# A memory-attention and FFN kernel: the second product of batches 2 to 7 in Strassen's form for every second pair of k blocks

## The chip, the cores and the metric

The kernel runs on one core of one Trainium2 chip. The metric is the device time of one execution in microseconds (us). The profile names the core's engines PE (TensorE: matrix products), PEld (its weight loads), DVE (VectorE), ACT (ScalarE), POOL (GpSimd) and SP (SyncE, which here only issues DMAs).

## What is computed

The inputs are q, k and v (8 batches, 8 heads, 576 tokens, 64 numbers a head), phi (32 memory slots a head) and two weight matrices, 512x2048 and 2048x512.

```python
a = phi - np.max(phi, axis=2, keepdims=True)
a = np.exp(a)
a = a / (np.sum(a, axis=2, keepdims=True) + 1e-09)
k_m = np.einsum('bhsm,bhsd->bhmd', a, k)
v_m = np.einsum('bhsm,bhsd->bhmd', a, v)
...
attn = attn / (np.sum(attn, axis=-1, keepdims=True) + 1e-09)
return np.matmul(attn, v_m).astype(np.float32)
...
h = x @ w_in
sp = np.maximum(h, 0.0) + np.log1p(np.exp(-np.abs(h)))
g = h * erf(sp)
return (g @ w_out).astype(np.float32)
```

x holds the attention's result, 4608 tokens by 512. `h = x @ w_in` is the first product and `g @ w_out` the second.

## The kernel before

**Stages.** The batches are worked off one after the other. For each, the kernel sums k and v under phi to 32 slots a head, and multiplies the slots of v with `w_in` beforehand (`vw`), so that the first product (`ffn1`) multiplies the softmax weights (`at`) of 256 slots with `vw`. Its 2048 columns are cut in 16 blocks k of 128, so that there are 128 steps (b, k) over the 8 batches.

**A step.** For one block k, `ffn1` makes h for the 576 tokens in two halves of 288 (`psh`); each half is copied from PSUM to SBUF by DVE or ACT (`h`). ACT makes softplus and erf (`e`), four steps at a time because each function needs its own table. `g_split` (L909) multiplies e by h on DVE (L932), rounds the result to `g_hi` (L934), keeps the rounding error as `g_lo` (L935), and POOL copies the last 64 tokens aside (L939). `ffn2` (L947) multiplies g with the rows k of `w_out`, which lie in SBUF as `wo` in a high and a low part; there are four blocks of 128 tokens, each with a PSUM bank (`pso0` to `pso3`) in which it sums over k.

**Three matmuls for a product.** A product of fp32 accuracy is made of three matmuls of the rounded parts (`products`, L843): high by high, high by low, low by high. So a block of 128 tokens takes three matmuls of 128x512 for each k.

**What is left of 576.** 576 is four times 128 and 64 more. `ffn2_rest` (L970) multiplies the last 64 tokens of two batches together, as one more block (`psr`), 16 k by three matmuls for each of four pairs of batches, 192 matmuls in all. The last block of the last batch is cut in two halves of 256 columns at its end (`last_block`, L988, `psy`).

**What sets the order.** The program is recorded as operations with a rank and with buffers from pools; `Plan.order` (L133) plays them through with a planned cost for each and writes the instructions of every engine in the order that results. A table at the end of the function shifts the ranks of single operations. On the chip each engine takes its instructions in that order, and waits where an input is not there. SP does the same with DMAs: a DMA whose buffer is not free holds up all that stand behind it.

**Pools.** h and e have five buffers each, `g_hi` and `g_lo` three each, the PSUM tiles of the first product share four banks (`ps`) with the attention's. `w_in` lies in SBUF for good (`w_in0` to `w_in3`, 1 MB each).

Of the kernel before, what the change touches and what calls it, by code (L numbers as in the profile page):

```python
# [250 lines left out]
def tile_memory_attention_then_erf_softplus_ffn(  # L251
# [22 lines left out]
    NB = U // 32  # L274
    NPR = DFF // 256
    NK = DFF // P
    NS = B * NK
    NT = S // P
    REST = S - NT * P
    NC = phi.shape[2]  # L280
    ROWS = [min(ROW, S - c * ROW) for c in range(NC)]
# [5 lines left out]
    ORDER = [(b, k) for b in range(B) for k in range(NK)]  # L287
    GROUPS = [4] * (NS // 4 - 1) + [2, 2]
    LAG = 6
# [4 lines left out]
    TAIL = 3  # L294
# [3 lines left out]
        for n, b, kw in (  # L298
            ("const", 1, {}),
            ("wo", NPR, {}),  # L300
            ("vw", 2, {}),
            ("att", 1, {}),
            ("at", 8, {}),
            ("small", 2, {}),
            ("el", 5, {}),
            ("g", 3, {}),
# [7 lines left out]
    room = {"wo": NPR, "vw_hi": 2, "vw_lo": 2, "at": 8, "h": HB, "e": EB}  # L314
    room.update({"g_hi": 3, "g_lo": 3, "raw": RAW, "ps": 4, "sc": 2, "dk": 1, "bias": 1, "phiT": 2, "row": 2})
# [6 lines left out]
        "h": ("el", [P, S], F32),  # L322
        "e": ("el", [P, S], F32),
        "sc": ("att", [P, NG, U], F32),
# [3 lines left out]
        **{n: ("small", [P, NG * NB], F32) for n in ("smx", "ssm", "srs")},  # L328
# [3 lines left out]
    def tile_(tag, *key, shape=None, dtype=F32, pool=None):  # L332
        key = plan.tile(tag, *key)
        p, s, d = SHAPES.get(tag, (pool, shape, dtype))
        T[key] = lambda: pools[p].tile(s, d, name=key[0], tag=tag, bufs=BUFS.get(tag))
        return key
# [21 lines left out]
    rest = const.tile([P, NK, 2, P], F32R, name="rest")  # L358
# [59 lines left out]
    def load_kv(rank, b, x, g):  # L418

        key = tile_("raw", "kv", b, x, g, shape=[P, NC, 4 * D], pool="raw")  # L420
        src = kv[b - 1, 2 * g + x] if b else kv_0[x, g]
        load(rank, P * NC * 4 * D * 4, [key], lambda: queue(b, g if x == 0 else 0).dma_start(out=get(key), in_=src))

    def load_q(rank, u):
        b, hf = divmod(u, 2)
        src = qT[b, hf].rearrange("r (p s) -> r p s", p=NP_)
        if u < 2:
            key = tile_("wo", "q", u, shape=[P, NP_, U], pool="wo")
            load(rank, P * NP_ * U * 4, [key], lambda: nc.sync.dma_start(out=get(key), in_=src))
            return  # L430
        for x in range(2):
            key = tile_("at", "q", u, x, shape=[P, 2, U], pool="at")
            load(rank, P * 2 * U * 4, [key], lambda x=x, key=key: nc.sync.dma_start(
                out=get(key), in_=src[:, 2 * x : 2 * x + 2]))
# [4 lines left out]
    def q_of(u, rows, p):  # L439
        return get(("q", u))[rows, p] if u < 2 else get(("q", u, p // 2))[rows, p % 2]  # L440

    wo, wf, raw_of = {}, {}, {}

    def decode(rank, name, c):
# [17 lines left out]
        if name == "in":  # L462
            dst = ("w_in", c)
# [5 lines left out]
        def merge():  # L469
            t, v = word(1), word(0)  # L470
            if name == "in":
                at_ = c % 2 * f
                to = w_in_sb[c // 2][:, :, at_ : at_ + f]
# [162 lines left out]
    def sums_and_turn(rank, b, part, rank_2=None, into=None):  # L636
# [11 lines left out]
        def sums_of(n):  # L648
# [4 lines left out]
            return get(banks[n])[:, U : U + n_x * D]  # L653
# [116 lines left out]
    def vw(rank, b, k, n, exact):  # L770
# [7 lines left out]
        ws = [(("w_in", k // 2), k % 2)] if n == 1 else [("w_in", c) for c in range(k // 2, (k + n) // 2)]  # L778
# [3 lines left out]
               lambda: of_heads(ps, vm[b % 2], lambda rows, p: w_in_sb[i][rows, p, cols]))  # L782
# [12 lines left out]
    def attention(rank, rank_2, u, more=0):  # L795
        b = u // 2
        s = tile_("sc", "sc", u)
        ps = heads(U + more, "sc", u)
        yield
        yield (4 * U / 2.4, [("km", b % 2)] + q_keys(u), [(k, "sc") for k in ps], [s],  # L800
               lambda: of_heads(ps, km[b % 2], lambda rows, p: q_of(u, rows, p), U))
# [4 lines left out]
        def wide(k):  # L806
            return get(k).unsqueeze(2).to_broadcast([P, NG * NB, M])

        for g in range(NG):
            op(DVE, on_dve(U), rank, [(ps[g], "sc")], [(s, g)], lambda g=g: nc.vector.transpose(  # L810
                out=get(s)[:, g, :], in_=get(ps[g])[:, :U]))
        mx, sm, rs = (tile_(n, n, u) for n in ("smx", "ssm", "srs"))
        op(DVE, on_dve(S), rank_2, [s], [mx], lambda: nc.vector.reduce_max(
            out=get(mx), in_=view(), axis=AX.X))
        op(DVE, on_dve(S), rank_2, [s, mx], [s], lambda: nc.vector.tensor_tensor(
            out=view(), in0=view(), in1=wide(mx), op=ALU.subtract))
        op(ACT, on_act(S), rank_2, [s], [s],
           lambda: nc.scalar.activation(get(s), get(s), AF.Exp, scale=SCALE if b >= TURNED else 1.0),
           kind="exp")
        op(DVE, on_dve(S), rank_2, [s], [sm], lambda: nc.vector.reduce_sum(  # L820
# [4 lines left out]
        op(DVE, on_dve(S), rank_2, [s, rs], [s], lambda: nc.vector.tensor_tensor(  # L825
            out=view(), in0=view(), in1=wide(rs), op=ALU.mult))
        shape = [P, NG, U]
        if u < 2:
            to = tile_("at", "at", u, shape=shape, pool="at")
        else:  # L830
            to = tile_("sc", "f", u)
        op(DVE, on_dve(S), rank_2, [s], [to], lambda: nc.vector.transpose(
# [4 lines left out]
    def at_split(rank, u, src):  # L837
        hi = tile_("at", "at_hi", u, shape=[P, NG, U], dtype=F32R, pool="at")
        lo = tile_("at", "at_lo", u, shape=[P, NG, U], dtype=F32R, pool="at")
        split(rank, hi, lo, src, S, lambda: get(hi), lambda: get(lo), lambda: get(src))  # L840
# [7 lines left out]
    def ffn1(rank, i, half):  # L848
# [5 lines left out]
        h = ("h", i)  # L854
        if i < IN_PSUM:
            ps = tile_(f"pso{half + 1}", "psh", i, half)
        else:
            if half == 0:
                tile_("h", *h)
# [19 lines left out]
        def keep():  # L879
            return get(h)[:, half * U : (half + 1) * U]  # L880

        op(DVE, on_dve(U), rank - 20, [ps], [(h, half)],
# [9 lines left out]
    def softplus(rank, i, edge):  # L892
        e = tile_("e", "e", i)
        if i < IN_PSUM:
            for x, (half, ps) in enumerate(halves_of(i)):
                last[:] = [op(ACT, on_act(U, True), rank, [ps], [(e, x)],
                              lambda half=half, ps=ps: nc.scalar.activation(
                                  get(e)[:, half], get(ps)[:, :U], AF.Softplus),
                              kind="softplus", edge=edge and x == 1, after=last)]
            return  # L900
        last[:] = [op(ACT, on_act(S), rank, [("h", i)], [e], lambda: nc.scalar.activation(  # L901
            get(e), get(("h", i)), AF.Softplus), kind="softplus", edge=edge, after=last)]

# [351 lines left out]
```

## Time and profile before

| what | value |
|---|---|
| time of three runs | 695.98 us median (695.84 to 696.05) |
| span of the profiled execution, first to last instruction | 694.3 us |
| what the median has beyond that span | 1.7 us |
| PE busy | 686.9 us, 99% |
| DVE busy | 460.5 us, 66% |
| ACT busy | 488.9 us, 70% |
| POOL busy | 117.0 us, 17% |
| DMA | 67.37 MB, 97 GB/s in the mean |

The profiled execution has no separate time of its own; its span is set against the median of the runs, which lie within 0.2 us. Busy times are unions of instruction spans. A matmul's span is longer than the distance to the next one, since they are pipelined, so that the distance from start to start, not the span, tells what a matmul costs in a row of them.

### The profile page before, as it was taken

How to read it: one execution, taken by the hardware profiler on the slowest of the kernel's cores; microseconds unless marked ns; L12 is line 12 of the kernel's file. 1: busy time of each engine (PE TensorE's matmuls, PEld its weight loads, DVE VectorE, ACT ScalarE, POOL GpSimd, SP SyncE). 2: the span in 40 equal slices, each digit the busy share in tenths (PEclk: the TensorE clock that was granted, in tenths of full speed). 3: DMA queues.
4: the chain of work that ended last, by engine and by line, in shares of the span. 5: the costliest groups of instructions: out<-in, count | busy, mean ns of one | idle time of the engine just before them, and what ended most of it. 6: DMA issues, size and time to landing. Idle time of an engine off the chain costs nothing.

```text
span 694.3 us, 12260 instructions
## 1 busy us (share of the span) xinstructions
PE 686.9 (99%) x4813; PEld 558.5 (80%) x4813; DVE 460.5 (66%) x807; ACT 488.9 (70%) x773; POOL 117.0 (17%) x262
## 2 busy tenths in 40 slices
PE   8999999999999999999999999999999999999998
PEld 4565778888887888888888888878888888888886
DVE  4999999678853587674863648774775346744560
ACT  3899999975876568867665776885576655757641
POOL 0021323132210222111111102111111011110120
PEclk9999999999999999999999999999999999999999
DMA  9999231624202151125211142110010100010002
GB/s 361 417 415 416 91 103 43 210 87 174 85 2 79 40 190 41 44 81 160 72 35 46 65 132 101 35 62 1 6 62 4 60 17 1 2 61 1 1 0 76
DMA packets 21433, 67.37 MB, mean 97 GB/s; under 512 B 3072, under 2 KB 3968, under 8 KB 21376
## 3 DMA queue, kind: packets, MB, share of 16 engines
q1 hardware_dynamic: 20944, 65.51, 26.3%
q10 hardware_dynamic: 432, 1.08, 0.4%
q8 instruction: 38, 0.62, 0.4%
q14 instruction: 19, 0.16, 0.1%
HBM read 57.14 MB, written 9.44 MB: 96 GB/s over the span
## 4 chain that ended last, share of the span: by engine, by line
PE 92%; DMA 2%; ACT 2%; DVE 2%; issue 1%; DVEq 0%
PE pso L943 50%; PE psh L866 28%; PE psr L943 6%; PE psa L762 5%; PE psa L671 2%; DMA q<-qT 2%; DVE w L457 1%; DMA phiT<-phiT 1%; DVE w_in L481 0%; ACT e L906 0%; DVE sc L810 0%; PE psy L943 0%; ACT e L901 0%; ACT L901 0%; ACT L529 0%
## 5 line engine op out<-in xcount | busy, mean ns | idle before, releaser
L943 PE MATMUL pso<-wo,g_hi 128*128 128x512 f32 x970 | 302.9, 393 | 0.0
L943 PEld LDWEIGHTS pso<-wo,g_hi 128*128 128x128 f32 x970 | 174.3, 188 | 41.8 <-issue 7.2
L943 PE MATMUL pso<-wo,g_lo 128*128 128x512 f32 x485 | 189.3, 390 | 0.0
L884 ACT ACTIVATE h<-psh 128x288 f32<-128x288 f32 x186 | 75.7, 409 | 123.5 <-PE psh L866 122.3
L939 POOL CAST rest<-g_hi 128x64 fp32r<-128x64 f32 x122 | 59.8, 491 | 417.4 <-DVE g_hi L934 406.1
L934 DVE CAST g_hi<-e 128x576 fp32r<-128x576 f32 x122 | 54.7, 452 | 83.5 <-PE pso L943 79.7
L866 PE MATMUL psh<-at_hi,vw_hi 128*128 128x288 f32 x496 | 107.9, 299 | 0.5 <-DVE sc L810 0.5
L943 PEld LDWEIGHTS pso<-wo,g_lo 128*128 128x128 f32 x485 | 91.1, 188 | 20.4
L866 PE MATMUL psh<-at_lo,vw_hi 128*128 128x288 f32 x496 | 106.6, 296 | 0.0
L866 PE MATMUL psh<-at_hi,vw_lo 128*128 128x288 f32 x496 | 105.5, 294 | 0.0
L932 DVE TENSOR_TENSOR e<-e,h 128x576 f32<-128x576 f32 x122 | 89.9, 754 | 18.8 <-ACT e L906 18.7
L866 PEld LDWEIGHTS psh<-at_hi,vw_hi 128*128 128x128 f32 x496 | 85.5, 188 | 17.1 <-DVE sc L810 4.9
L935 DVE TENSOR_TENSOR g_lo<-e,g_hi 128x576 fp32r<-128x576 f32 x122 | 93.8, 772 | 7.0
L901 ACT ACTIVATE e<-h 128x576 f32<-128x576 f32 x127 | 86.3, 685 | 9.7 <-DVE g_lo L935 6.6
L906 ACT ACTIVATE e<-e 128x576 f32<-128x576 f32 x128 | 81.0, 678 | 0.4
L866 PEld LDWEIGHTS psh<-at_hi,vw_lo 128*128 128x128 f32 x496 | 80.3, 189 | 0.0
L866 PEld LDWEIGHTS psh<-at_lo,vw_hi 128*128 128x128 f32 x496 | 79.1, 188 | 0.0
L939 POOL CAST rest<-g_lo 128x64 fp32r<-128x64 f32 x122 | 50.1, 412 | 88.4 <-DVE g_lo L935 81.8
L373 DVE TENSOR_TENSOR vw_lo<-psa,vw_hi 128x512 fp32r<-128x512 f32 (+1 forms) x64 | 40.6, 667 | 11.4 <-ACT vw_hi L371 11.3
L943 PE MATMUL psr<-wo,rest 128*128 128x512 f32 x192 | 46.0, 389 | 0.0
L906 ACT ACT_TABLE_LOAD x33 | 42.3, 1283 | 0.6
L901 ACT ACT_TABLE_LOAD x32 | 41.1, 1283 | 2.4 <-DVE g_lo L935 1.8
(90 smaller groups left out, 622.7 us busy)
## 6 DMA issues: line engine op xcount, KB each, us to landing
kv<-kv SPq DMA_DIRECT2D x31, 640.0 KB, 8.5
w<-w_in SPq DMA_DIRECT2D x8, 1023.8 KB, 14.9
w<-w_out SPq DMA_DIRECT2D x8, 1023.8 KB, 14.1
q<-qT SPq DMA_DIRECT2D x28, 288.0 KB, 3.3
out<-ot SPq DMA_DIRECT2D x31, 256.0 KB, 2.2
phi<-phi SPq DMA_DIRECT2D x7, 640.0 KB, 4.8
phiT<-phiT SPq DMA_DIRECT2D x15, 288.0 KB, 2.9
q<-qT SPq DMA_DIRECT2D x2, 576.0 KB, 10.3
```

Source lines behind the costliest of these rows:

```text
L373: lambda: nc.vector.tensor_tensor(out=get_lo(), in0=get_src(), in1=get_hi().bitcast(F32), op=ALU.subtract))
L671: nc.tensor.matmul(out=sums_of(n)[M * j : M * (j + 1)], lhsT=get(a)[at_c, c, h * M : (h + 1) * M], rhs=get(kv_of)[at_c, c, at_ * w : (at_ ...
L762: nc.tensor.matmul(out=get(ps[par])[p * M : (p + 1) * M, :n], lhsT=w[rows, p, :], rhs=x_of(rows, p), start=True, stop=True,)
L866: nc.tensor.matmul(out=get(ps)[:, :U], lhsT=x[:, g, k % 4 * P : (k % 4 + 1) * P], rhs=y[:, g, :], start=(n + g == 0), stop=(n == len(parts ...
L884: other={ACT: (on_act(U, True), lambda: nc.scalar.activation(keep(), get(ps), AF.Identity))})
L901: last[:] = [op(ACT, on_act(S), rank, [("h", i)], [e], lambda: nc.scalar.activation(get(e), get(("h", i)), AF.Softplus), kind="softplus", ...
L906: last[:] = [op(ACT, on_act(S), rank, [e], [e], lambda: nc.scalar.activation(get(e), get(e), AF.Erf), kind="erf", edge=edge, after=last)]
L932: op(DVE, on_dve(S), rank, [e, h], [e], lambda: nc.vector.tensor_tensor(out=get(e), in0=get(e), in1=get(h), op=ALU.mult))
L934: op(DVE, on_dve(S, 1), rank, [e], [hi], lambda: nc.vector.tensor_copy(out=get(hi), in_=get(e)))
L935: op(DVE, on_dve(S), rank, [e, hi], [lo], lambda: nc.vector.tensor_tensor(out=get(lo), in0=get(e), in1=get(hi).bitcast(F32), op=ALU.subtract))
L939: lambda x=x, y=y: nc.gpsimd.tensor_copy(out=rest[:, k, x, cols], in_=get(y)[:, NT * P :]))
L943: nc.tensor.matmul(out=o, lhsT=y, rhs=z, start=(start and n == 0), stop=(stop and n == len(parts) - 1))
```

## The change

**Work in half batches.** Batches 0 and 1 are as before, up to their last 64 tokens. From batch 2 on the unit is a half batch (256 tokens first, then 320) and a pair c of k blocks (k = 2c and 2c + 1). `RUNS` lists the 96 units; the second half takes the pairs in the order 7 to 0. `ffn1_pair` makes h of both k into one tile `he`, which holds e in front of it; e, h and the sums below share its room. There are 7 such tiles for h and e together.

**Seven products.** For a pair, the second product is a 2x2 block product: two blocks of 128 tokens by two k blocks, times two k blocks by two halves of 256 columns of `wo`. For pairs with odd c it is done with seven block products of 128x256 (`PRODUCTS`, 21 matmuls of 256 columns); for even c (`SKIP`) it is done directly with four of 128x512 (`DIRECT`, 12 matmuls of 512 columns). The seven need sums and differences of blocks on either side. On g's side DVE makes them in three additions (`operands`), after which high and low parts of 896 or 960 columns are made; with a direct pair these are 512 columns. On the weights' side `combine` makes them once, in batch 1, for the four odd pairs, and a DMA puts them to DRAM (`sums_away`); each use loads them again (`ty`, 1 MB, into three places `q8`, which `w_in`'s quarters share). The four accumulators (`acc`) are combined at the end of a half batch by one ACT copy and five or six additions on DVE (`finish_pair`).

**Leftovers.** 64 tokens of each batch go to DRAM by DMA (`rest_away`) and come back as blocks of four batches (`g_rest`): two blocks of 128 tokens and all 16 k, after batch 3 and at the end, with the same two forms. `ffn2_rest`, `last_block` and POOL's copies of `g_hi` and `g_lo` go.

**To DRAM and back.** `w_in`'s four quarters are put to DRAM once and are loaded again for each batch (`win`); the first quarter of `vw` of each batch from 2 on too (`vw_away`). The table of ranks is made anew (388 entries, 56 before), and 56 operations (4 before) are tied to DVE or to ACT.

```diff
-    RAW = 5
-    HB, EB = 5, 5
+    RAW = 4
+    HB, QB, AB, FB = 7, 3, 6, 3
...
-    LAG = 6
+    LAG, LAG2, PAUSE = 6, 7, 5
...
+    SKIP, SKIP_REST = (0, 2, 4, 6), (0, 2, 4, 6)
...
-    w_in_sb = [const.tile([P, NP_, 512], F32, name=f"w_in{p}") for p in range(4)]
...
+    w_in_away = [away(f"w_in_away{p}", [P, NP_, 512]) for p in range(4)]
+    sums_away = [away(f"sums_away{c}", [P, 2, 4, HALF]) for c in range(NPR)]
...
+    def operands(rank, name, gf, w, fast):
...
+        if fast:
+            op(DVE, on_dve(2 * P), rank, [g], h, lambda: nc.vector.tensor_tensor(
+                out=blocks(col(s1), 2, P), in0=blocks(col(0), 2, pitch), in1=blocks(col(w), 2, pitch), op=ALU.add))
+            op(DVE, on_dve(P), rank, [g] + h, h, lambda: nc.vector.tensor_tensor(
+                out=col(s2), in0=col(s1), in1=col(pitch), op=ALU.subtract))
+            op(DVE, on_dve(2 * P), rank, [g] + h, h, lambda: nc.vector.tensor_tensor(
+                out=blocks(col(s2 + P), 2, P), in0=blocks(col(pitch), 2, s1 + P - pitch), in1=blocks(col(0), 2, s1),
+                op=ALU.subtract))
...
+        op(ACT, on_act(run), rank, both, [hi], lambda: nc.scalar.activation(like(hi), of(), AF.Identity),
+           other={DVE: (on_dve(run, 1), lambda: nc.vector.tensor_copy(out=like(hi), in_=of()))})
+        op(DVE, on_dve(run), rank, both + [hi], [lo], lambda: nc.vector.tensor_tensor(
+            out=like(lo), in0=of(), in1=like(hi).bitcast(F32), op=ALU.subtract))
...
+    PRODUCTS = ((0, "a11", 0, 0), (0, "s2", 3, None), (1, "s1", 0, None), (1, "s3", 1, None),
+                (2, "a12", 1, 0), (2, "s4", 1, 1), (3, "a22", 2, None))
+    DIRECT = ((2, 1, 0), (2, 3, 1), (3, 0, 0), (3, 2, 1))
...
+            n = to.stop - to.start
+            op(PE, 3 * mm(n, False), rank, [hi, lo, t if j is None else wo[c], acc], [acc], emit)
...
+        op(ACT, on_act(DM, True), rank, [a[0]], [t[0]],
+           lambda: nc.scalar.activation(part(0, 0, 2), bank(0, 0, 2), AF.Identity))
+        add(1, 1, [t[0]], [(t[0], 1)], lambda: part(0, 1), lambda: part(0, 0), lambda: part(0, 1))
+        add(2, 1, [a[1], c12], [c21], lambda: part(1, 0), lambda: bank(1, 1), lambda: part(0, 1))
+        add(3, 1, [a[1], c12], [c12], lambda: part(0, 1), lambda: bank(1, 0), lambda: part(0, 1))
+        add(4, 1, [a[1], c21], [c22], lambda: part(1, 1), lambda: bank(1, 0), lambda: part(1, 0))
+        add(5, 2, [a[2], t[0]], [t[0]], lambda: part(0, 0, 2), lambda: bank(2, 0, 2), lambda: part(0, 0, 2))
...
+            def again(n=n, c=c, t=t):
+                tile_("q8", *t, shape=[P, 2, 4, HALF], dtype=F32R, pool="q8")
+                fetch(at(n + WHEN["ty"]), t, lambda: get(t).bitcast(F32), sums_away[c], P * 8 * HALF * 4)
```

**What stands where.** The first place is PE's second product in the middle of the program. Before, one k of one batch is four blocks (`pso`), each with three matmuls of 512 columns:

```order
L943 MATMUL pso_3290<-wo_1244,g_hi_3327 128x512 x2
L943 MATMUL pso_3290<-wo_1244,g_lo_3333 128x512
L943 MATMUL pso_3355<-wo_1244,g_hi_3327 128x512 x2
L943 MATMUL pso_3355<-wo_1244,g_lo_3333 128x512
L943 MATMUL pso_3360<-wo_1244,g_hi_3327 128x512 x2
L943 MATMUL pso_3360<-wo_1244,g_lo_3333 128x512
```

Now, in batch 4, the rows of one bank (`acc_4126`): two of the seven products of an odd pair (`wo_915`), then two of the four of an even one (`wo_944`):

```order
L1139 MATMUL acc_4126<-wo_915,g_hi_4169 128x256 x2
L1139 MATMUL acc_4126<-wo_915,g_lo_4177 128x256
L1139 MATMUL acc_4126<-wo_915,g_hi_4169 128x256 x2
L1139 MATMUL acc_4126<-wo_915,g_lo_4177 128x256
L1139 MATMUL acc_4126<-wo_944,g_hi_4235 128x512 x2
L1139 MATMUL acc_4126<-wo_944,g_lo_4240 128x512
L1139 MATMUL acc_4126<-wo_944,g_hi_4235 128x512 x2
L1139 MATMUL acc_4126<-wo_944,g_lo_4240 128x512
```

Over the whole program PE's matmuls of the second product of rounded parts go from 1647 of 512 columns and 18 of 256 to 984 of 512 and 1176 of 256; the first product keeps its number (1488, of 288 columns before, now 336 of 288, 576 of 256 and 576 of 320).

The second place is DVE towards the end of batch 0. Before, around the 10th `g_lo` (L935):

```order
L932 TENSOR_TENSOR e<-e,h 128x576
L373 TENSOR_TENSOR vw_lo<-psa,vw_hi 128x512
L373 TENSOR_TENSOR wo<-wf,wo 128x1024
L934 CAST g_hi<-e 128x576
L511 TENSOR_REDUCE pmx<-phiT 128x1
L935 TENSOR_TENSOR g_lo<-e,g_hi 128x576
L883 COPY h<-psh 128x288 x2
L531 TENSOR_SCALAR psm<-psm 128x1
L562 TENSOR_TENSOR phi<-phi,psa 128x1280
```

Now, ahead of the 8th `g_lo` (L978), which is the last row here:

```order
L387 TENSOR_TENSOR vw_lo<-psa,vw_hi 128x512 x2
L850 TENSOR_TENSOR sc<-sc,smx 128x576
L387 TENSOR_TENSOR wo<-w,wo 128x1024
L592 TENSOR_TENSOR phi<-phi,psa 128x1280
L855 TENSOR_REDUCE ssm<-sc 128x18
L975 TENSOR_TENSOR he<-he 128x576
L857 TENSOR_SCALAR ssm<-ssm 128x18
L919 COPY he<-psh 128x288
L859 RECIPROCAL srs<-ssm 128x18
L977 CAST g_hi<-he 128x576
L860 TENSOR_TENSOR sc<-sc,srs 128x576
L978 TENSOR_TENSOR g_lo<-he,g_hi 128x576
```

The addition to phi (L562, now L592) has moved from behind the 10th `g_lo` to ahead of the 8th. Up to the 9th, DVE has one such addition and one `vw_lo` of 512 more than before, and one `pmx` reduction less.

The third place is SP's queue in batch 2 (`_N` are numbers of tiles). Before, at a like place, SP only loads inputs and stores results:

```order
L416 DMA phi_1519<-phi 128x1280
L422 DMA kv_1521<-kv 128x1280
L422 DMA kv_1523<-kv 128x1280
L422 DMA kv_1525<-kv 128x1280
L422 DMA kv_1527<-kv 128x1280
L1022 DMA out<-ot_1548 128x512
```

Now the load of the weights' sums for c = 7 (`ty_2737`) stands behind three DMAs to `rest_away`:

```order
L466 DMA win_2616<-w_in_away0_103 128x2048
L466 DMA win_2637<-w_in_away1_104 128x2048
L548 DMA bias_2653<-row_2590 128x256
L462 DMA rest_away0_7_122<-he_2466 256x1x64
L462 DMA rest_away0_6_121<-he_2504 256x1x64
L462 DMA rest_away0_5_120<-he_2574 256x1x64
L466 DMA ty_2737<-sums_away7_114 128x2048
```

It goes to the place that `win_2616` leaves. On PE the last matmul that reads `win_2616` stands 21 rows ahead of the first that reads `ty_2737`, and between them are 9 matmuls of 256 columns, 24 of 320 and 3 of 512.

## Rows read from the trace of the kernel before

**Rows 1.** The page's first and fourth part: span, busy engines, the chain's shares.
```profile
span 694.3 us, 12260 instructions
PE 686.9 (99%) x4813; PEld 558.5 (80%) x4813; DVE 460.5 (66%) x807; ACT 488.9 (70%) x773; POOL 117.0 (17%) x262
...
PE 92%; DMA 2%; ACT 2%; DVE 2%; issue 1%; DVEq 0%
```

**Rows 2.** Busy time by stretch: stretch, length, then PE, PEld, DVE, ACT, POOL, clock, DMA.
```profile
20.00:60.00 40.00, 39.03 (x278) 23.45 (x272) 38.90 (x55) 38.23 (x61) 5.69 (x10) 1.00 1.02 415
...
20.00:128.00 108.00, 106.97 (x757) 77.23 (x756) 106.72 (x160) 101.68 (x160) 24.69 (x37) 1.00 0.60 233
128.00:180.00 52.00, 52.00 (x426) 43.16 (x426) 39.73 (x76) 39.94 (x64) 11.08 (x19) 1.00 0.47 165
180.00:690.00 510.00, 509.46 (x3395) 428.00 (x3394) 303.35 (x550) 339.36 (x534) 80.49 (x200) 1.00 0.15 50
```

**Rows 3.** PE's timeline near the end: start, span, instruction, count.
```profile
685.99 0.39 PE L943 MATMUL pso<-wo,g_lo 128*128 128x512 f32 x1
...
686.67 0.39 PE L943 MATMUL pso<-wo,g_lo 128*128 128x512 f32 x1
...
688.94 0.40 PE L943 MATMUL psy<-wo,g_hi 128*128 128x256 f32 x2
...
690.97 0.28 PE L943 MATMUL psy<-wo,g_lo 128*128 128x256 f32 x1
```

**Rows 4.** PE's timeline in the middle: two rows of the first product.
```profile
300.67 0.42 PE L866 MATMUL psh<-at_hi,vw_hi 128*128 128x288 f32 x2
300.94 0.43 PE L866 MATMUL psh<-at_lo,vw_hi 128*128 128x288 f32 x2
```

**Rows 5.** Groups by line: busy time, mean ns of one, idle time before.
```profile
L943 PE MATMUL pso<-wo,g_hi 128*128 128x512 f32 x970 | 302.9, 393 | 0.0
...
L943 PE MATMUL pso<-wo,g_lo 128*128 128x512 f32 x485 | 189.3, 390 | 0.0
```

**Rows 6.** DVE's timeline where it works without a gap.
```profile
267.80 0.42 DVE L934 CAST g_hi<-e 128x576 fp32r<-128x576 f32 x1
268.13 0.75 DVE L932 TENSOR_TENSOR e<-e,h 128x576 f32<-128x576 f32 x1
268.80 0.79 DVE L373 TENSOR_TENSOR at_lo<-f,at_hi 128x576 fp32r<-128x576 f32 x1
```

**Rows 7.** Groups by line: DVE's durations at other widths.
```profile
L373 DVE TENSOR_TENSOR wo<-w,wo 128x1024 fp32r<-128x1024 f32 x7 | 8.6, 1225 | 0.0
...
L562 DVE TENSOR_TENSOR phi<-phi,psa 128x1280 f32<-128x1280 f32 x2 | 3.0, 1481 | 0.0
...
L1010 DVE TENSOR_TENSOR ot<-ot,psy 128x256 f32<-128x256 f32 x2 | 0.8, 422 | 13.9 <-PE psy L943 13.9
...
L998 DVE COPY ot<-pso 128x512 f32<-128x512 f32 x1 | 0.7, 691 | 3.5 <-PE pso L943 3.5
```

**Rows 8.** Timelines of DVE and PEld at the 9th g_lo.
```profile
113.51 0.79 DVE L935 TENSOR_TENSOR g_lo<-e,g_hi 128x576 fp32r<-128x576 f32 x1
...
114.58 0.19 PEld L943 LDWEIGHTS pso<-wo,g_lo 128*128 128x128 f32 x1
```

**Rows 9.** DMA issues: KB each, median us to landing; first of 115 to 122 us.
```profile
kv<-kv SPq DMA_DIRECT2D x1, 640.0 KB, 3.8
...
w<-w_in SPq DMA_DIRECT2D x8, 1023.8 KB, 14.9
...
out<-ot SPq DMA_DIRECT2D x9, 128.0 KB, 2.4
...
out<-ot ACTq DMA_DIRECT2D x1, 128.0 KB, 1.7
```

**Rows 10.** Timeline of the program's last two steps.
```profile
691.29 0.42 DVE L1010 TENSOR_TENSOR ot<-ot,psy 128x256 f32<-128x256 f32 x1 [0.65 <-PE psy L943]
...
691.74 0.35 ACTq L1012 DMA_DIRECT2D out<-ot  x1
```

More of the change, by code (lines that the diff above doesn't have):

```diff
@@ new lines, in erf, with rest_of @@
+    def erf(rank, i, edge, n=S):
+        he, e = ("he", i), (("he", i), "e")
+        last[:] = [op(ACT, on_act(n), rank, [e], [e], lambda: nc.scalar.activation(
+            get(he)[:, :n], get(he)[:, :n], AF.Erf), kind="erf", edge=edge, after=last)]
+    def rest_of(rank, i, t, read):
+        b, k = ORDER[i]
+        st = ("rst", b, k // 2)
+        if k % 2 == 0:
+            tile_("rst", *st, shape=[P, 2, REST], pool="small")
+        op(POOL, 400, rank, [read], [(st, k % 2)], lambda: nc.gpsimd.tensor_copy(
+            out=get(st)[:, k % 2], in_=get(t)[:, NT * P : S]))
+        if k % 2:
+            r, slot = divmod(b, RUN)
+            put(rank + 60, [st], rest_away[r][k // 2][:, :, slot], lambda: get(st), P * 2 * REST * 4)
@@ new lines, in g_pair @@
+    def g_pair(rank, n, fast):
+        b, x, c = RUNS[n]
+        he, w = ("he", n + NS), width(2 * b + x)
+        op(DVE, on_dve(2 * w), rank, [(he, "e"), (he, "h0"), (he, "h1")], [(he, "e")], lambda: nc.vector.tensor_tensor(
+            out=get(he)[:, : 2 * w], in0=get(he)[:, : 2 * w], in1=get(he)[:, 2 * w : 4 * w], op=ALU.mult))
+        operands(rank, (n + NS,), he, w, fast)
+        if x:
+            r, slot = divmod(b, RUN)
+            put(rank, [(he, "e")], rest_away[r][c][:, :, slot],
+                lambda: blocks(get(he)[:, P : P + REST], 2, w), P * 2 * REST * 4)
@@ L1033, in tile_memory_attention_then_erf_softplus_ffn @@
         for k in range(first, first + n):
[L1034 to L1036 removed]
+            split_at[k] = max(ends[-1] + 1, k + 4)
+            second[k] = k + LAG
     TOGETHER = [tuple((g, x) for g in range(NG) for x in range(2))]
@@ L1150, in tile_memory_attention_then_erf_softplus_ffn @@
+    for m, c in enumerate(c for c in range(NPR) if c not in SKIP or c not in SKIP_REST):
+        n = NK + WHEN["combine"] + 2 * m
+        when(n, combine, at(n), c)
     for k in range(NS):
@@ L1157, in tile_memory_attention_then_erf_softplus_ffn @@
+    groups = [n for n in range(N) if n % 4 == 3]
+    second_kinds = (ffn2, ffn2_pair, finish_pair)
+    length = int(max(x[0] for x in work)) + 2
+    starts = {step(n): n for n in range(N)}
+    for i in range(length):
+        n = starts.get(i)
         if i < NS:
@@ L1199, in tile_memory_attention_then_erf_softplus_ffn @@
             issued[y.engine] = y
+        for k in x.placed:
+            p = plan.pool_of[k]
+            if not callable(T[k]) and k not in taken:
+                taken.add(k)
+                if p in taker and taker[p].engine != made[x][0].engine:
+                    tc.add_manual_dep(made[x][0], taker[p].name, near, reason="order of places")
+                taker[p] = made[x][0]
 def kernel(q, k, v, phi, moe_w_in, moe_w_out):
```

506 lines of the change are left out of this document (324 added, 182 removed), and 53 rows, old and new, of tables (g, of).

## The prediction

> **What bounds the kernel now.** I read the page's busy times and the chain first: PE has 686.9 of 694.3 us and 92% of the chain [rows 1]. A busy matmul engine is not yet one at its pace, so the next view is the timeline: three matmuls of 128x512 take 686.67 - 685.99 = 0.68 us, 226.7 ns each from start to start [rows 3], in the middle of the program as at its end. The 1455 matmuls of the main blocks [rows 5], the 192 of `psr` and the 18 of `psy` are the second product: 1647 x 226.7 ns + 18 x 119.4 ns = 375.5 us, more than half of the span. The windows show the rest: PE has 509.46 of 510 us from 180 to 690, at a granted clock of 1.00, which is the 2.4 GHz level, while DVE has 303.35 and ACT 339.36 [rows 2]. So after 180 us only matmuls count. From 20 to 128 us it is different: DVE has 106.72 of 108 us, so there PE and DVE end together. The 9th `g_lo` ends at 113.51 + 0.79 = 114.30, and PE loads it as weights at 114.58 [rows 8]; DVE is ahead by 0.28 us.
>
> **Matmuls: -12.0 us.** The 18 `psy` matmuls are the second width: (690.97 - 688.94) / 17 = 119.4 ns for 256 columns, each with a weight load of its own [rows 3]. The line through both widths gives 132.8 ns for 288 columns; the rows say 0.27 us for two [rows 4], so it holds. By the order, 663 matmuls of 512 and 18 of 256 go (152.4 us), and 1176 of 256 come (140.4 us): -12.0 us. That is 0.213 us for each of the 56 odd pairs (21 x 119.4 against 12 x 226.7 ns), not an eighth of a pair's 2.72 us, since the seven products are 21 matmuls with 12 ns beyond their columns each, against 12. The first product has the same columns in the same number of matmuls: 0. The bundles of small matmuls go from 32 to 33 and cost some 0.1 us on each side: +0.2.
>
> **DVE as a whole: dearer, but covered.** In a row of independent operations DVE takes 268.80 - 268.13 = 0.67 us from start to start for 576 elements and 0.33 for a cast [rows 6]; a tensor operation of n elements so takes about n / 0.96 + 70 ns. With this price the rows that the change adds are: sums on g's side 56 x (0.34 + 0.20 + 0.34) = 49; low parts of 512, 896 and 960 in place of 576: +27; the ends of half batches +34 (70 additions of 256 or 512 from or to PSUM, 14 of 256 in SBUF); weights' sums 4 x 3.6 = 14 (price of 1024: 1225 ns less the overlap of some 85) [rows 7]; copies +4; casts -9, since ACT takes 51 of them. Together some +121 us: 460.5 becomes 581 of 684, 85%. ACT's share stays near its 70% (fewer, wider copies, 12 table loads less, but 51 casts). POOL's casts go away, which the chain does not name. DVE from 180 us on: 303 + 107 = 410 of 500 us. So the mean leaves PE the bound; the price is in places where DVE's work comes in lumps.
>
> **Where DVE comes too late: +1.1 and +0.8 us.** In the first 108 us DVE has no reserve. Up to the 9th `g_lo` it has one addition to phi (1.41 us without overlap [rows 7]) and one `vw_lo` (0.61) more and one `pmx` (0.67) less: 1.3 us later, with 0.28 in hand and PE itself some tenths earlier: +1.1. The weights' sums come behind that, in batch 1. At the 17th `g_lo` DVE has 10.5 us more behind it than before, and had 12.4 in hand there by the same count, so they are hidden; without that reserve they would cost 10.5. For batches 2 to 7 I set DVE's rows between two splits against PE's rows from the release of the g places (three) to the use of the later split, for all of them: the smallest reserve is 0.5 us at start-to-start prices. At full durations, 13% more, shortfalls of 2.4, 1.6 and 2.4 us come out in three places. Bounds so 0 and 6.4; I take 0.8, near the first, since a row of operations shows the overlap [rows 6].
>
> **The loads of the weights' sums: +1.5 us.** Each of the 45 is 1 MB, needs a place that an earlier tile leaves, and PE stops at its first matmul if it is late. Counted on PE's order from the last reader of a place to the first of the new tile, nine have 5.2 to 7.3 us, the others more. For `ty_2737` that is 9 x 119.4 + 24 x 146 + 3 x 226.7 ns = 5.3 us. The nearest row is a load of 640 KB alone, 3.8 us [rows 9]; the missing 384 KB at 415 GB/s [rows 2] make it 4.7, an estimate. So a load that starts at once is 0.5 us early, and one that stands behind another transfer of 256 to 640 KB (0.6 to 1.6 us) is up to 1 us late. Bounds: 0, and nine times 1.6 less 0.5, 10 us; I take 1.5. Queued behind such a load on SP are the next loads of `w_in`, q and kv, and the stores, of which `w_in`'s have 7.5 us of lead and more. In PE's order everything stands behind it.
>
> **The end: +1.3 us.** After the last matmul came an addition of 256 (0.42 us [rows 10]) and one store of 128 KB on ACT's queue (1.7 us [rows 9]). Now it is an addition of 512 (0.69 [rows 7]) and two stores of 128 KB, one after the other on SP: 0.35 for the second issue [rows 10] and 2.4 in place of 1.7. Sum +1.3, at least +0.3.
>
> **Sum.** -12.0 + 0.2 + 1.1 + 0.8 + 1.5 + 1.3 = -7.1 us. The profiled span of 694.3 becomes 687.2; with the 1.7 us that the median has beyond it, 688.9. With all low ends (only the end's 0.3 and the bundles' 0.2 left) it is 684.5; with the high ends of the two kinds of waits (+5.6 and +8.5), 703.
>
> **The rivals.**
> - *DVE's operations do not overlap where they depend on one another.* The sums on g's side are a chain on one tile, and the ends of half batches another. Then the 6.4 us of shortfalls come in full, with 1 to 2 in batch 0: 694.5 to 695.5. For it: such a chain stands in no row of before. Against it: the order sets other work between most links. The Trainium skill (VectorE: DVE Perf Modes, "The DRAIN you can't avoid") has each next operation wait until the pipe is empty, which by itself would be this case; the trace differs for independent ones, where a 0.75 us operation is followed after 0.67 us.
> - *The loads are late as a rule* (the other side). SP's queue is in order: `ty_2737` stands behind three DMAs to `rest_away` that wait for DVE (the third place in the order), and each of these writes rows of 256 bytes, of which no row of before has a price. If a load takes longer than its lead by d in each of the 12 half batches' two tightest places, it costs 24 d; the gain of 8.6 that is left without this term is used up at d = 0.36 us. The crowded queue of the start has 14.9 us for 1 MB [rows 9]. At d = 0.8 the time is 707. Against it: from 180 us on the DMA engines are 15% busy [rows 2], and the change adds some 106 MB to 67, 250 GB/s in the mean of the 415 that the start shows.
> - *A matmul of 256 columns costs more in a mixed stream* than in the 18 in a row. The change is even at 129.5 ns (12 x 226.7 / 21), ten above the row; then nothing is gained and the waits leave some +5: 701. The Trainium skill (TensorE: Matmul & The Clock Gate, "Back-to-back issue gap") gives a sustained 81 ns at 128 columns and 131 at 512; on the line between, 98 at 256, a fast pair would take 2.06 us against 1.57, and 56 of them would add 27 us: some 728. The rows here bear out neither value: 119.4 and 226.7, proportional to columns but for 12 ns.
>
> **Chances.** The forecast's case (684.5 to 692): 0.60. DVE's chains at full price (692 to 696): 0.19. Loads late, 696 to 715: 0.15. The dearer 256: 0.03. Under 684.5, if waits of before go too: 0.03. What a measurement of this kernel can tell from no change is 0.2%, 1.4 us: under 694.6 is faster. 0.60 + 0.03 and most of the second case, with a few late loads, make 0.80 faster; 0.07 the same; 0.13 slower. The range for 8 in 10 is 684.3 to 697.5; the forecast's own is 684.5 to 692.
>
> **What would show it.** Right: PE near 99% with 0.119 us from start to start in `acc<-ty` rows; DVE at 82 to 88%; no wait of PE over 1.5 us after 180 us; the 9th `g_lo` about 1 us later against PE. Wrong: waits of PE on `ty` in the waits' view (loads), on `g_lo` or on `ot` (DVE), or 256 columns above 125 ns among others. The forecast falls if one of the first two adds up to more than 8 us.

## The result, and the profile after

The changed kernel takes 699.68 us in the median of six runs (697.6 to 702.25), the kernel before 696.0 (695.84 to 696.05): 1.0058 times as long in the ratio of the means, 95% interval 1.004 to 1.0075. It is slower by 0.6%, where 688.9 us and faster were forecast; the range ended at 697.5. The profiled run took 699.62 us with a span of 697.5.

The page of the changed kernel, first and fourth part, answers to [rows 1]:

```profile
span 697.5 us, 13618 instructions
PE 680.0 (97%) x5308; PEld 573.3 (82%) x5308; DVE 574.8 (82%) x1055; ACT 494.3 (71%) x757; POOL 22.8 (3%) x38
...
PE 86%; DMA 10%; DVE 2%; ACT 1%; issue 0%; SPq 0%; DVEq 0%
```

PE has less to do than before, as forecast, and DVE has about the work that was expected (574.8 us, 581 forecast). But PE is no longer busy all the time, and DMA holds 10% of the chain where it held 2%. The windows say where, with the columns of [rows 2]:

```profile
20.00:128.00 108.00, 106.89 (x768) 75.11 (x762) 104.15 (x152) 98.86 (x161) 13.95 (x20) 1.00 0.74 294
180.00:690.00 510.00, 501.28 (x3949) 444.35 (x3942) 410.56 (x793) 343.65 (x516) 0.00 (x0) 1.00 0.67 231
```

From 180 us on PE lacks 8.7 of 510 us, against 0.5 before, and the DMA engines are 67% busy instead of 15%. The waits of PE name the transfers (total, times, longest):

```profile
PE acc L1139 <- DMA ty<-sums_away: 5.5, 6, 1.6
PE psa L792 <- DMA win<-w_in_away: 2.5, 2, 1.8
...
PE acc L1139 <- DVE g_lo L1092: 0.3, 1, 0.3
```

Seven loads of the weights' sums stand in the chain of what ended last (start, time to landing); four of them:

```profile
233.60 6.26 DMA ty<-sums_away
...
326.18 7.82 DMA ty<-sums_away
...
512.05 9.14 DMA ty<-sums_away
...
582.96 8.87 DMA ty<-sums_away
```

The medians of the DMA issues (KB each, us to landing), and SP's timeline around the load of 512.05, show what made 6 to 9 us of the 4.7 that a load takes alone:

```profile
ty<-sums_away SPq DMA_DIRECT2D x45, 1024.0 KB, 6.3
win<-w_in_away SPq DMA_DIRECT2D x28, 1024.0 KB, 7.3
```

```profile
503.24 0.33 SPq L466 DMA_DIRECT2D ty<-sums_away  x1
503.63 1.44 SPq L462 DMA_DIRECT2D rest_away<-he  x2
...
507.16 0.38 SPq L466 DMA_DIRECT2D win<-w_in_away  x1
507.64 0.38 SPq L462 DMA_DIRECT2D vw_away<-vw_hi  x1
508.11 0.40 SPq L462 DMA_DIRECT2D vw_away<-vw_lo  x1
512.05 0.32 SPq L466 DMA_DIRECT2D ty<-sums_away  x1
```

The part on queues of the DMA view, for 325 to 342 us alone, where the loads of 326 and 337 are under way (packets, MB, share of 16 engines):

```profile
q1 hardware_dynamic: 2152, 5.29, 100.7%
```

By PE's rows, each late load was issued within 0.6 us of its place coming free. What the one at 512.05 had ahead of it in flight was not one transfer of 256 to 640 KB but 1 MB of `w_in` and two writes of 512 KB of `vw`, all issued in the 5 us before. The trace has them landing in the order of issue: `w_in` at 516.08, the writes at 517.63 and 518.61, this load at 521.19, so that of its 9.14 us some 2.6 passed after the last one ahead of it had landed. At such places the DMA engines are full or nearly so (94% busy from 495 to 525 us).

The other rows that the forecast rests on came out nearly as expected. PE's timeline at the end, to be read as [rows 3]: 0.36 us for three matmuls of 256 columns on `ty` (688.26 to 688.62), 0.12 from start to start, in the mixed stream too.

```profile
688.26 0.40 PE L1139 MATMUL acc<-ty,g_hi 128*128 128x256 f32 x2
688.50 0.28 PE L1139 MATMUL acc<-ty,g_lo 128*128 128x256 f32 x1
688.62 0.40 PE L1139 MATMUL acc<-ty,g_hi 128*128 128x256 f32 x2
```

Of DVE's timeline the 9th `g_lo`, 0.71 us later than in [rows 8] (1.3 were counted), and the last addition:

```profile
114.22 0.79 DVE L978 TENSOR_TENSOR g_lo<-he,g_hi 128x576 fp32r<-128x576 f32 x1
...
693.03 0.69 DVE L1160 TENSOR_TENSOR ot<-acc,ot 128x512 f32<-128x512 f32 x1 [1.05 <-PE acc L1139]
```

### The profile page after: what moved, and what is told of

The parts are those of the page before. It is cut to its first block, busy times and chain, and to the rows that moved or that the text cites. A ratio compares the mean times of both kernels' runs of the same rounds, so it can differ in the third digit from the quotient of the medians.

```text
span 697.5 us, 13618 instructions
## 1 busy us (share of the span) xinstructions
PE 680.0 (97%) x5308; PEld 573.3 (82%) x5308; DVE 574.8 (82%) x1055; ACT 494.3 (71%) x757; POOL 22.8 (3%) x38
## 2 busy tenths in 40 slices
DMA packets 56127, 173.37 MB, mean 249 GB/s; under 512 B 22400, under 2 KB 23040, under 8 KB 45696
## 4 chain that ended last, share of the span: by engine, by line
PE 86%; DMA 10%; DVE 2%; ACT 1%; issue 0%; SPq 0%; DVEq 0%
PE acc L1139 38%; PE psh L1040 21%; PE pso L984 13%; DMA ty<-sums_away 8%; PE psh L902 7%; PE psa L792 5%; PE psa L701 2%; DMA q<-qT 2%; DMA phiT<-phiT 1%; DVE sc L845 0%; DVE he L1098 0%; DVE g L969 0%; ACT L943 0%; ACT he L938 0%; DVE w L484 0%
## 5 line engine op out<-in xcount | busy, mean ns | idle before, releaser
L1139 PE MATMUL acc<-wo,g_hi 128*128 128x512 f32 (+1 forms) x784 | 205.4, 348 | 0.1
L1139 PEld LDWEIGHTS acc<-wo,g_hi 128*128 128x128 f32 x784 | 132.8, 190 | 21.6 <-issue 7.0
L1139 PE MATMUL acc<-wo,g_lo 128*128 128x256 f32 (+1 forms) x392 | 134.9, 344 | 0.3 <-DVE g_lo L1092 0.3
L1092 DVE TENSOR_TENSOR g_lo<-he,g_hi 128x512 fp32r<-128x512 f32 (+2 forms) x112 | 98.9, 897 | 4.1 <-ACT g_hi L1090 1.7
L938 ACT ACTIVATE he<-he 128x512 f32<-128x512 f32 (+2 forms) x127 | 85.0, 683 | 11.5 <-DVE he L1056 5.6
L1139 PE MATMUL acc<-ty,g_hi 128*128 128x256 f32 x448 | 87.2, 285 | 5.6 <-DMA ty<-sums_away 5.5
L1040 PE MATMUL psh<-at_hi,vw_hi 128*128 128x320 f32 (+1 forms) x384 | 82.4, 296 | 0.2 <-DVE sc L845 0.2
L1040 PE MATMUL psh<-at_lo,vw_hi 128*128 128x320 f32 (+1 forms) x384 | 82.4, 296 | 0.0
L1040 PE MATMUL psh<-at_hi,vw_lo 128*128 128x320 f32 (+1 forms) x384 | 82.4, 296 | 0.0
L943 ACT ACTIVATE he<-he 128x512 f32<-128x512 f32 (+2 forms) x128 | 80.8, 676 | 0.4
L984 PE MATMUL pso<-wo,g_hi 128*128 128x512 f32 x208 | 65.7, 397 | 0.0
```

The costliest lines, as they stand in the source:

```text
L938: last[:] = [op(ACT, on_act(n), rank, [(he, "h0"), (he, "h1")], [(he, "e")], lambda: nc.scalar.activation(get(he)[:, :n], get(he)[:, n : 2 ...
L943: last[:] = [op(ACT, on_act(n), rank, [e], [e], lambda: nc.scalar.activation(get(he)[:, :n], get(he)[:, :n], AF.Erf), kind="erf", edge=edg ...
L984: nc.tensor.matmul(out=o, lhsT=y, rhs=z, start=(start and n == 0), stop=(stop and n == len(parts) - 1))
L1040: nc.tensor.matmul(out=get(ps[j])[:, o : o + w], lhsT=y[:, g, k % 4 * P : (k % 4 + 1) * P], rhs=z[:, g, :], start=(m + g == 0), stop=(m == ...
L1092: op(DVE, on_dve(run), rank, both + [hi], [lo], lambda: nc.vector.tensor_tensor(out=like(lo), in0=of(), in1=like(hi).bitcast(F32), op=ALU. ...
L1139: nc.tensor.matmul(out=get(acc)[:, to], lhsT=y, rhs=z, start=(first and q == 0), stop=(last and q == 2), skip_group_check=True)
```

## Three theories

T1: PE waits for loads. A load of 1 MB is issued when its place comes free, and then shares the DMA engines with what else is in flight; its lead of 5 to 7 us is too short for that. T2: DVE's dearer work sets PE back. T3: PE's work itself is dearer (256 columns, small bundles). The kernel before took 695.98 to 696.03 us beside each group of runs; the intervals are those of the ratio to it.

| run | us | ratio, interval |
|---|---|---|
| e1, a quarter of the sums' bytes | 693.24 | 0.9963 (0.9951 to 0.9976) |
| e2, without the sums on g's side | 702.35 | 1.0092 (1.0079 to 1.0106) |
| e3, sums' loads in four parts | 707.13 | 1.0159 (1.0145 to 1.0172) |
| e4, a quarter of both loads' bytes | 688.5 | 0.9894 (0.9879 to 0.9909) |
| e5, writes of `vw` later | 694.99 | 0.9986 (0.9978 to 0.9995) |
| e6, sums ahead of `w_in` | 698.61 | 1.0035 (1.0022 to 1.0048) |
| e7, e5 and e6 | 695.38 | 0.9993 (0.9981 to 1.0006) |
| e8, sums' loads on POOL's queue | 705.98 | 1.0133 (1.0118 to 1.0147) |
| e9, e5, three of e6's exchanges, `phiT` first | 691.99 | 0.9942 (0.9929 to 0.9954) |
| e10, e9 with `phiT`, then sums, then `w_in` | 691.09 | 0.9932 (0.992 to 0.9945) |
| e11, e4 with four products for seven | 699.65 | 1.0054 (1.0041 to 1.0066) |
| e12, e4 and e2 | 687.92 | 0.9888 (0.9873 to 0.9903) |

## Experiments: which of the three theories

**e1 and e4: a quarter of the bytes.** The branch for `win` is e4's alone; there the products of v's slots read part 0 of it.

```diff
-        op(SP, 60, rank, [("away", of.name)], [key], lambda: nc.sync.dma_start(out=to(), in_=of),
+            if key[0] == "ty":
+                nc.sync.dma_start(out=to()[:, :, :1], in_=of[:, :, :1])
+            elif key[0] == "win":
+                nc.sync.dma_start(out=to()[:, :1], in_=of[:, :1])
...
-                    b = [get(t)[:, z, i] for z in range(2)]
+                    b = [get(t)[:, z, 0] for z in range(2)]
```

> Each of the 45 loads of the weights' sums brings 256 KB in place of 1 MB, and the products with sums all read that quarter (three quarters of the sums are so left out of the computation); every instruction of PE, DVE and ACT stays in its place. Theory T1 (PE waits because a load is issued only when its place comes free and then stands behind 1 MB transfers): the 5.5 us of PE's wait on `ty` fall under 0.5, the waits on `w_in`'s quarters shrink too since 35 MB of 173 go; 692.5 to 694.5 us, and the runs lie closer together than the 4.7 us of the changed kernel. Theory T2 (DVE's dearer work sets PE back): 699 to 700. Theory T3 (PE itself is dearer: the pitch of 512 columns, more small bundles): 699 to 700.

> As the first of these four, and the 28 reloads of `w_in`'s quarters bring 256 KB in place of 1 MB too, with the products of v's slots from batch 1 on reading that part (so three quarters of `w_in` are left out there). T1: against the first, the waits on `w_in`'s loads (2.5 us in the changed kernel) go as well: 1 to 2.5 us less, 690.5 to 693, which is 6.5 to 9 under the changed kernel. T2 and T3: 699 to 700.

e1 saves 6.4 us, as T1 says, and e4 11.2, some 2 more than T1's figure, both with PE's and DVE's instructions where they were. The waits' view had shown 8.0 of these 11.2; it counts as idle only what lies behind a matmul's modelled end, which is later than the start that the next one would have had. In e1 PE's waits on `ty` are gone and those on `w_in` stay:

```profile
PE psa L796 <- DMA win<-w_in_away: 2.8, 2, 1.5
```

In e4 there are none on either; its issues and its window:

```profile
ty<-sums_away SPq DMA_DIRECT2D x45, 256.0 KB, 3.1
...
win<-w_in_away SPq DMA_DIRECT2D x28, 256.0 KB, 3.9
```

```profile
180.00:690.00 510.00, 501.42 (x3954) 446.41 (x3954) 411.95 (x797) 342.99 (x516) 0.00 (x0) 1.00 0.41 131
```

This window holds some 8 us without matmuls at its end, since the last one ends at 681.7: up to 681 us PE lacks 0.3 of 501. What is left at 688.5 us is the change without its late loads. e4 also has all the writes of 256-byte rows to `rest_away`, on which the prediction's second rival laid weight, and they alone make nothing late.

**e2 and e12: DVE without its three additions.** The e2 edit is made on the changed kernel, that of e12 on e4.

```diff
+        sums = name[0] == "rest"
         if fast:
-            op(DVE, on_dve(2 * P), rank, [g], h, lambda: nc.vector.tensor_tensor(
+            op(DVE, on_dve(2 * P), rank, [g], h, lambda: sums and nc.vector.tensor_tensor(
```

> The three additions on g's side are left out for the fast pairs of the half batches (the leftovers' blocks keep them), so that the low and high parts are made of room that holds e and h; the order of all that is left is the same. DVE has some 43 us less. T1: PE's waits on the loads stay, 698.5 to 700 us. T2: the time falls with DVE's load, by 3 us or more, to 693 to 697. T3: no change.

> Base is the run with a quarter of the bytes of both loads (688.5 us); the three additions on g's side of the half batches' odd pairs are left out too, as in the second run. Here no load is late, so that DVE's dearer work shows by itself. T2: if DVE's chains hold PE, 1 to 6 us less, 682.5 to 687.5. T1: DVE is covered, 688 to 689.

The busy times of e12, where e4 has 574.0 us on DVE:

```profile
PE 677.6 (99%) x5308; PEld 574.0 (84%) x5308; DVE 538.5 (79%) x911; ACT 493.4 (72%) x757; POOL 28.0 (4%) x38
```

With 35.5 us less on DVE, e12 is 0.6 us under e4, and the two intervals overlap: the three additions are covered. What else DVE has more was not taken out; no wait of PE on DVE in e4 is over 0.3 us. So T2 explains next to nothing of the miss. e2 is a miss for all theories: 2.7 us slower with less work. Its waits and three windows, with the columns of [rows 2], show what happened in the profiled run:

```profile
PE acc L1140 <- DMA ty<-sums_away: 8.2, 6, 3.1
```

```profile
332.00:336.00 4.00, 0.65 (x2) 0.45 (x3) 4.00 (x11) 0.04 (x1) 0.00 (x0) 0.86 1.06 293
336.00:340.00 4.00, 4.00 (x18) 3.81 (x19) 2.85 (x6) 1.52 (x2) 0.00 (x0) 0.50 0.88 252
340.00:344.00 4.00, 4.00 (x30) 2.93 (x36) 1.31 (x2) 0.63 (x1) 0.00 (x0) 0.79 0.57 189
```

PE stood still for 3.35 of the 4 us to 336, and the granted clock fell to 0.50, which is the 1.2 GHz level, through the next window and partly in those beside it. In the second and third window, where PE worked all the time, missing clock of 0.50 and 0.21 times 4 us is some 2.8 us of work lost, on top of the wait. The mean clocks of e2's four runs, 0.995 to 0.998, lie under those of four of the changed kernel's six (0.999 to 1.0), so that a good part of the 2.7 us can be clock. Why the load at that place came later than in the changed kernel is not settled.

**e11: what the seven products bring.** On e4, odd pairs do four products of 512 columns, one in each bank.

```diff
+                if t is not None:
+                    if m:
+                        return
+                    a, to, j = 0, slice(0, DM), bank % 2
-                if t is None:
+                if t is None or m == 0:
                     b = [get(wo[c])[:, z, j] for z in range(2)]
```

> Base is the run with a quarter of the bytes of both loads (688.5 us). In the 56 odd pairs the seven products are left out and four of 512 columns stand in their place, one in each bank, on parts of the same g and without reading the sums (the sums on both sides are still made and loaded); the order of all engines is the same. If a pair of seven gains 0.213 us against four (the term of -12.0 us), the time is 688.5 + 11.9 = 700.4; T3 (256 columns dearer in the mixed stream than in a row) would give less than 9 us more, under 697.5.

It takes 11.15 us more than e4, 0.199 us for each of the 56 pairs against 0.213 forecast. T3 falls as the cause: the products of 256 columns bring nearly what they should.

## Experiments: how a load comes to be late

**e3: four parts.**

```diff
+            if key[0] == "ty":
+                for i in (3, 0, 1, 2):
+                    nc.sync.dma_start(out=to()[:, :, i], in_=of[:, :, i])
```

> Each load of the weights' sums is issued as four DMAs of 256 KB in the order of first use (i = 3, 0, 1, 2). The whole kernel is computed. T1: a late load now holds PE only until its first quarter has landed, some three quarters of the 2.5 us that its own bytes take sooner, for about seven late loads: 3 to 5 us less if later quarters keep ahead of PE, 695 to 697.5; a gain of nothing if four pieces of 1 KB a row cost more than they save. T2 and T3: 699 to 700.

A miss by some 10 us. PE's wait on `ty` did shrink, to 0.7 us, but SP's timeline and the waits show the price:

```profile
325.43 3.02 SPq L469 DMA_DIRECT2D ty<-sums_away  x4
```

```profile
PE psa L797 <- DMA win<-w_in_away: 4.9, 2, 2.9
PE acc L1144 <- DVE g_lo L1097: 2.8, 3, 2.0
PE acc L1144 <- DVE ot L1165: 1.5, 1, 1.5
```

Four issues take SP 3.02 us, one took 0.32 to 0.60, and all that stands behind on SP is later by that; and the packets grow from 56127 to 98609. The Trainium skill (DMA: Bandwidth & Descriptors, "Bandwidth") asks for 1 MiB or more in one DMA; the run goes the same way, with 7.4 us lost to the changed kernel. How much of that is SP's time and how much the smaller packets was not taken apart.

**e8: another queue.**

```diff
+            by = nc.gpsimd if key[0] == "ty" else nc.sync
+            by.dma_start(out=to(), in_=of)
```

> Whole computation; the 45 loads of the weights' sums are issued by POOL, on a queue of its own, all else in SP's. If a late load is late since it stands behind earlier transfers in one queue, it now shares the DMA engines with them and lands sooner, and the loads of `w_in` land later: 695 to 698. If the sum of bytes in flight is what counts, whatever the queue, 699 to 700. If a load costs more by this queue (a longer way from issue to landing), the waits on `ty` grow: over 702.

The time is that of the third case, and PE's waits on `ty` grow as it says, but its reason, a longer way for each load, shows little: 6.5 us in the median, 6.3 before. A load takes no shorter on its own queue:

```profile
ty<-sums_away POOLq DMA_DIRECT2D x45, 1024.0 KB, 6.5
```

```profile
PE acc L1141 <- DMA ty<-sums_away: 7.5, 4, 3.9
```

The Trainium skill (DMA: Bandwidth & Descriptors, "Issuing engines are not separate DMA queues") says that transfers of all issuers run on the same 16 engines and interleave; the medians agree. PE's longest wait grew from 1.6 to 3.9 us. The load behind it was issued at 327.87 and took 10.54 us, where SP's was issued at 326.18 and took 7.82; why is open.

**e5 to e7: the same bytes in another order.** The plan's list is changed after it is made; PE, DVE, ACT and POOL keep their order. The numbers are places in the plan's list. e5:

```diff
-    for x in plan.order():
+    out_ = plan.order()
...
+    late = {x: y for x, y in [(1042, 1142), (1108, 1142), (1479, 1591), (1510, 1591), (2326, 2371), (2331, 2371)]}
+    behind = {y: [out_[x] for x in late if late[x] == y] for y in late.values()}
+    out_ = [z for n, x in enumerate(out_) for z in ([] if n in late else [x]) + behind.get(n, [])]
+    for x in out_:
```

e6 has in place of this, and e7 ahead of it:

```diff
+    for x, y in [(993, 1033), (1454, 1469), (2281, 2306), (1981, 1982), (2665, 2666)]:
+        out_[x], out_[y] = out_[y], out_[x]
```

> Whole computation; every engine's order as in the changed kernel, only SP's is changed: the six writes of the first quarter of `vw` to DRAM in batches 3, 4 and 6 (512 KB each), which nobody waits for within 35 us but which stand in the queue at the late loads, are issued 6 to 26 us later. T1 says that what a late load shares the DMA engines with is the cause: the loads of the weights' sums at 326, 337, 503 and 512 us then land 1 to 2 us earlier each, in all 2 to 4 us less, 695.5 to 697.5. A theory by which a late load is late for the moment at which its place comes free alone gives no change, 699 to 700.

> Whole computation; in five places SP's queue has a load of the weights' sums ahead of the load of a quarter of `w_in` that stood up to four DMAs ahead of it and is used 8 us later or more; the two change places in the room as well, so that the sums' load gets the place that comes free 0.7 to 9 us earlier. T1: the waits at 233, 326, 433, 503 and 583 us go (about 1 us each), 1 to 2.5 us may come back where the quarter of `w_in` is late in its turn; 695 to 697.5. T2 and T3: 699 to 700.

> Whole computation; the two changes of SP's order together. T1: PE's waits on the two kinds of loads, 8.0 us in the profile of the changed kernel, fall under 2.5; 692 to 694.5 us, faster than the kernel before (696.0). It can't come under the 688.5 of the run with a quarter of the bytes. If contention only moves from one load to the next: 696 to 699.

e5 alone gives 4.7 us, more than expected: six writes that nobody waits for soon were in the way. e6 gives 1.1, less than expected and not clear of noise (its interval and the changed kernel's overlap), and e7, between its two cases, no more than e5. The waits of e5, e6 and e7, in this order:

```profile
PE psa L792 <- DMA win<-w_in_away: 1.3, 2, 1.0
PE acc L1139 <- DVE g_lo L1092: 1.3, 1, 1.3
PE acc L1139 <- DMA ty<-sums_away: 0.9, 2, 0.7
```

```profile
PE psa L792 <- DMA win<-w_in_away: 4.9, 2, 3.0
PE acc L1139 <- DVE g_lo L1092: 1.8, 1, 1.8
PE acc L1139 <- DMA ty<-sums_away: 1.7, 1, 1.7
```

```profile
PE psa L792 <- DMA win<-w_in_away: 3.1, 2, 2.5
```

In e6 and e7 the wait has gone over to `w_in`. In e5 a wait on DVE appears, and DVE's timeline there leads back to a transfer again:

```profile
504.50 0.75 DVE L541 TENSOR_REDUCE pmx<-phiT 128x1 f32<-128x576 f32 x1 [2.06 <-DMA phiT<-phiT]
505.17 1.28 DVE L387 TENSOR_TENSOR vw_lo<-psa,vw_hi 128x512 fp32r<-128x512 f32 x2
...
506.43 1.15 DVE L1092 TENSOR_TENSOR g_lo<-he,g_hi 128x960 fp32r<-128x960 f32 x1
```

DVE stood 2.06 us for `phiT`, issued 0.4 us behind 1 MB of `w_in`, and the `g_lo` that PE needs stood behind it.

**e9 and e10: `phiT` first.** As e7, but with other exchanges; e9 keeps (993, 1033), (1981, 1982) and (2665, 2666) and adds (1454, 1455) and (2281, 2283). e10 also has (1455, 1469) and (2283, 2306), which puts `phiT`, the sums and `w_in` in this order.

> Whole computation; the writes later as in the fifth run, three of the five exchanges of the sixth (at 233, 433 and 583 us, where the quarter of `w_in` has time), and at 322 and 496 us the load of a `phiT` half, for which DVE waits with nothing in hand, goes ahead of the quarter of `w_in` that was issued 0.4 us before it. T1: against the fifth run (695.0) the wait of PE on DVE's low part at 507 us (1.4 us), which stood behind that `phiT`, and the small waits at 233, 433 and 583 go; 692.5 to 694.5 us. If the loads only push each other about: 694.5 to 696.

> As the ninth run, with the sums' loads at 326 and 503 us also ahead of the quarter of `w_in` before them, right behind `phiT`. T1: the wait on the sums' load at 332 us (1.0) goes, and the quarters of `w_in` used at 338 and 512 us are late by 0.6 to 2.5 us as in the seventh run: 693 to 696, no better than the ninth.

Both came out under their ranges, by 0.5 and 1.9 us, and beat the kernel before: 691.99 and 691.09 us, 0.6% and 0.7% under it. Their intervals overlap, so that e10's two exchanges more are not shown to help. The chain's shares of e10 and its SP around the same place as above:

```profile
PE 92%; DMA 4%; DVE 2%; ACT 1%; issue 0%; DVEq 0%; SPq 0%
```

```profile
493.09 0.33 SPq L426 DMA_DIRECT2D phiT<-phiT  x1
493.83 0.33 SPq L466 DMA_DIRECT2D ty<-sums_away  x1
...
498.84 0.49 SPq L466 DMA_DIRECT2D win<-w_in_away  x1
...
506.71 0.32 SPq L466 DMA_DIRECT2D ty<-sums_away  x1
...
510.61 0.39 SPq L462 DMA_DIRECT2D vw_away<-vw_hi  x1
```

`phiT` and the sums are issued ahead of `w_in`, and the writes behind all of them; the waits' view of this run names neither load. It carries all the bytes, and is 2.6 us from e4.

## Why the prediction was wrong

**The step that failed** is "The loads of the weights' sums: +1.5 us". The lead of 5.3 us for `ty_2737` was right (issued at 233.60, needed about 238.8: it landed at 239.86, after a wait of 1.1 from start to start), and so was the 4.7 us of a load alone. The sentence that failed is that a late one "stands behind another transfer of 256 to 640 KB" and is up to 1 us late. Ahead of the one at 512.05 stood a 1 MB load and two 512 KB writes of `vw`, and the seven late loads took 6.3 to 9.1 us. The writes to `vw_away` and their place in SP's queue were in the change, and the working didn't price them. It also let `w_in`'s loads pass with "7.5 us of lead and more", where they take 7.3 in the median. With the loads small, the time is 688.5 (e4): the two kinds of loads cost 11.2 us, 6.4 on the sums (e1) and 4.7 more on `w_in`. So the term of 1.5 us measured 6.4, still inside its own bounds of 0 and 10, and the loads of `w_in`, which stood at nothing, measured 4.7. The mean of 250 GB/s of 415, held against lateness, was right and said nothing about single places: the DMA engines are 67% busy in the mean from 180 us on and full from 325 to 342.

**Without the loads** the sum gives 687.4, and e4 has 688.5. That it comes so near is in part luck, since the errors below go both ways; 0.4 us more lie in what the runs have beyond the profiled span (2.1 us, 1.7 before).

**Matmuls, -12.0**: nearly right. e11 shows 11.15 for the 11.9 in the odd pairs. Added up from start to start over PE's rows of the profiled runs, all of the second product's matmuls of rounded parts went from 380.1 to 369.0 us. The Trainium skill (TensorE: Matmul & The Clock Gate, "Back-to-back issue gap"), from whose figures the prediction estimated 728, is not borne out by the 0.12 us of the mixed stream. The first product, priced at 0, takes some tenths of a us to 1.2 more, by how the gaps in its rows are counted (199.8 to 200.4 with all of them), and the second product's exact matmuls of batch 0, which the sum left out, take 1.2 more (19.5 to 20.7).

**DVE too late, +1.1 and +0.8**: too large. PE's only wait on `g_lo` is 0.3 us, and e12 leaves 0.6 for the additions. The rival's premise is nevertheless true where a link of the chain directly follows the other. Here the second addition (L1072) reads what the first (L1070) writes:

```profile
294.21 0.42 DVE L1070 TENSOR_TENSOR he<-he 128x256 f32<-128x256 f32 x1
294.66 0.29 DVE L1072 TENSOR_TENSOR he<-he 128x128 f32<-128x128 f32 x1
```

It starts 0.45 us after the first, behind its end, while independent operations of this width follow after 0.33 to 0.34. But these two stand so in only 6 of the 56 chains. The rival's time fell since the order sets other work between the links, as the prediction's argument against it said, and the bound near 0 was the right one.

**The end, +1.3**: the time from the last matmul's end to the end of the span went from 3.05 to 4.5 us.

**The rival** "loads late as a rule" was right in that loads exceed their lead, with too small a chance (0.15). But the late loads were issued within 0.6 us of their place coming free, so the DMAs to `rest_away` ahead of them in SP's queue did not hold them back for long, and its price was not 24 times d: seven late loads cost 0.4 to 1.8 us each and two of `w_in` about as much. DVE's wait on `phiT`, which no case had, came out once these were shorter (1.3 us of PE in e5).

## What to carry to other kernels

A load with a lead near its own time is priced by what is in flight when it starts, not by the mean share of the DMA engines: write down the queue's order around each tight load, and count every transfer of the 5 us ahead of it, writes too. Put what nobody waits for soon behind what somebody waits for: six writes issued 6 to 23 us later were worth 4.7 us, while cutting the load in parts, or giving it a queue of its own, made it worse. When a wait is taken away, look for the next transfer in the same queue (here `w_in`, then `phiT` by way of DVE).

## What the hardware showed besides

In e2 a long wait of PE cost twice: after 3.35 us without work the clock was granted at 0.50 for some us, and some 2.8 us of work were lost beside the wait. In e3 the clock's mean is 0.97 in the windows of 360 to 420 and of 480 to 540 us, and the mean clocks of the changed kernel's six runs go with their times (0.999 to 1.0 in those of 697.6 to 699.75 us, 0.995 and 0.996 in those of 702.25 and 701.7). The run to run spread, 4.7 us against 0.2 before, goes with the loads: with a quarter of their bytes (e4, four runs) it is 0.7.
